# An attention and gated feed-forward block on one Trainium2 core: the second query block ends in half-width passes too, and the last one consists of them

## The chip, the cores and the metric

The kernel runs on one core of a Trainium2 chip. The metric is the device time of one execution in microseconds (us), as the median of several runs; lower is better. One execution was also taken by the hardware profiler, and its trace is what the text reads.

## The reference

One sequence of 2048 rows with 640 columns goes through a pre-normalized attention with 32 heads of 20 columns, and then through a gated feed-forward part with 1728 inner columns, all in bf16:

```python
qkv = (layernorm(x) @ wqkv)                      # 640 -> 3 x 640, 32 heads of 20
p = softmax(q @ k.T * 20 ** -0.5)                # per head, 2048 x 2048
h = x + (p @ v) @ wo
g, u = layernorm(h) @ w_gate, layernorm(h) @ w_up
h2 = h + (g * u) @ w_down
```

## The kernel before

**Attention.** The 32 heads are kept in 8 head groups (`NG`) of four, each head in a slot of 32 rows, so that four heads' score matmuls fill the 128 rows of TensorE. The 2048 queries are four blocks of 512 (`QB`), called 0 to 3. A *segment* is one head group's attention over all 16 key tiles for one *pass*, and a pass is a range of query columns: "0" to "3" are whole blocks, "C" and "D" are the two halves (256 columns, `HW`) of block 2, and "A" and "B" those of block 3. Blocks 0 and 1 are done in whole segments. Blocks 2 and 3 do their first two head groups (`SPLIT_G`) whole and the other six first for the left and then for the right half. Block 0's first four groups are done in four pieces of keys each, since the projections are still running then.

The segments' score columns are strung together and cut into *score tiles* of 1536 columns (three PSUM banks, `EW`); there are 683, the last one of 1024. The main loop runs over score tiles. For each, `emit_S` writes the score matmuls (L518), lets ScalarE take the Exp (L532) and may first let VectorE take the third bank with a polynomial of four instructions (`emit_x`, L562, L572, L573, L567), so that ScalarE's call is only 1024 columns wide. `x_takes` decides on that: the tile must lie in one segment and at least two tiles ahead of that segment's end, VectorE must not be behind by the planner's own clock, and in block 3 `room()` must find that the work still outstanding fits behind the remaining tiles. `emit_AV` (L716) multiplies the exponentials with the values some tiles later into one accumulator, which VectorE copies to `asb` (L728) when a segment ends.

**Normalizing.** A segment's sums of exponentials are inverted and spread over the rows of `asb` in one of two ways. `norm` goes by DRAM, with seven DMAs on SP's queue: `sums` (L616), `sums_all` (L617), and after a reciprocal on VectorE `scr` (L629) and four of `bc` (L632); POOL then multiplies (L638). `job_norm`, for the segments in `FAST`, goes by small matmuls on TensorE (L646, L662).

**The tail of a part.** When all head groups of a part (a whole block, or its left or right half) are normalized, `add_tail` queues its output projection (`job_out`: L953, with the sums for the second layer norm in `ln2_pieces`, then transposes into `ln2T`), the gated part (`job_glu`: `glu_sum` L1026 for 512 columns, `glu_pair` L1044 for 256 columns) and the down projection (`job_y`: L1090, four steps of 14 matmuls for two row tiles). Weights of the gated part come in seven slices of 256 columns; each is a pair of DMAs (`wu` and `wg`, L999, 320 KB each) into two buffers per name, called for one slice ahead of use. For block 3, slices 3 to 6 stay in the room that the queries leave free (`load_res`).

**Order.** All of this is put in order while the program is written. The planner keeps clocks of its own (`at`), and `run_job` fills the time that TensorE has left between two score tiles with steps of the queued jobs; `spare` does so with VectorE's steps (`aux`). `urgent` jobs go first. Where TensorE would be idle for long, `keep_warm` (L484) and `cool` (L514) write matmuls whose results nobody reads. Rows of `x` for a part are loaded early (`rows_early`) when the parts in `HELD_BY` have been stored. Each engine executes its own instructions in the order in which they were written, and so does SP with its DMAs.

**The end.** The tail of block 3's left half runs among the score tiles of its right half; what is left of it then is done in `last_tail`, which holds one of its four down projection steps back on purpose (`held`) and puts all leftovers (`fill()`) where TensorE waits for the last layer norm. Its order on TensorE is: output projection of the last two row tiles (`out_most`, L1188 and L1190) with the last normalization (L646, L662) in between, the leftovers (L1090), two transposes (L275), the gated part (L1026), and the down projection (L1090).

```python
    while i < n_tiles or av_q:
        ...
            rows_early(*due[0][2:])
        while due and normed(...):
            add_tail(*due.pop(0)[2:])
        if i < n_tiles:
            ran = run_job(max(at["exp"] - S_EXP - MARGIN, at["slot"][-2]))
```

Of the kernel before, what the change touches and what calls it, by code (L numbers as in the profile page):

```python
# [21 lines left out]
D = 640  # L22
H = 32
DH = 20
NT = S // P
# [4 lines left out]
NG = H // HPG  # L30
# [5 lines left out]
HW = QB // 2  # L36
# [3 lines left out]
FP = 7  # L40
FPW = 256
G1 = 4
SPLIT_G = 2
QA = 3 * QB
RES0 = 3
SM_SCALE = float(DH) ** -0.5
# [7 lines left out]
WAIT = "not yet"  # L54
# [27 lines left out]
def kernel(  # L82
# [17 lines left out]
    pool = lambda name, bufs=1, **kw: ctx.enter_context(tc.tile_pool(name=name, bufs=bufs, **kw))  # L100
# [44 lines left out]
    now = {"i": 0, "forced": False}  # L145
# [48 lines left out]
    def bn(mv, k, src, halves=None):  # L194
        st = small.tile([P, 2, 6], F32, name="st", bufs=4)
        for h in range(2):
            nc.vector.bn_stats(st[:, h, :], halves[h] if halves else src[:, h * HALF:(h + 1) * HALF])  # L197
        nc.vector.bn_aggr(mv[:, k, :], st[:])
# [39 lines left out]
    def ln_apply(dst, src, m32, r, k):  # L238
        nc.vector.tensor_scalar(dst, src, m32[:, k:k + 1], r[:, k:k + 1], ALU.subtract, ALU.mult)
# [17 lines left out]
    def evac(eng, dst, src):  # L257
        if eng == "act":
            nc.scalar.copy(dst, src)
        else:  # L260
            dve(690 if dst.dtype == BF16 and len(dst.shape) == 2 else 490)
            nc.vector.tensor_copy(dst, src)  # L262

    end = {"pool": None}

    def bank(dt=F32, w=BANK):
        if end["pool"] is None:
            return mip.tile([P, w], dt, name="mi", tag="mi")
        ps = end["pool"].tile([P, BANK], F32, name="f", tag="f")
        return ps if dt == F32 else ps[:].bitcast(dt)[:, 0:w]  # L270

    def job_T(ln, dst, eng="dve", ps=None, after=None):
        ps = bank(BF16, D) if ps is None else ps
        for c in range(KT):
            nc.tensor.transpose(ps[:, c * P:(c + 1) * P], ln[:, c * P:(c + 1) * P], ident[:])  # L275
        if after:
            after()
        evac(eng, dst, ps[:].rearrange("p (c k) -> p c k", k=P))
        yield 60 * KT
# [26 lines left out]
    def job_V(t, half):  # L306
        ps = bank()
        for c in range(KT):
# [8 lines left out]


    PASS = {"0": (0, 0, QB), "1": (1, 0, QB), "2": (2, 0, QB), "3": (3, 0, QB),
            "C": (2, 0, HW), "D": (2, HW, HW), "A": (3, 0, HW), "B": (3, HW, HW)}  # L320
    segs = []
    for ch in range(NB):
        for g in range(G1):
            kind = "copy" if ch == 0 else "last" if ch == NB - 1 else "add"
            segs.append(("0", g, ch * TPB, (ch + 1) * TPB, kind))
    segs += [("0", g, 0, NT, "only") for g in range(G1, NG)]
    segs += [("1", g, 0, NT, "only") for g in range(NG)]
    for full, halves in ("2", "CD"), ("3", "AB"):
        segs += [(full, g, 0, NT, "only") for g in range(SPLIT_G)]
        segs += [(p, g, 0, NT, "only") for p in halves for g in range(SPLIT_G, NG)]  # L330
    FINAL = len(segs) - 1
    TAILS = {0: [0], 1: [0], 2: [0, 2]}
    FAST = {("C", NG - 1), ("D", NG - 1), ("A", NG - 1), ("B", NG - 2)}

    tiles, cur_t, pos = [], [], 0
    for s, (p, g, lo, hi, _) in enumerate(segs):
# [23 lines left out]
    done = set()  # L360
# [4 lines left out]
    aux = deque()  # L365
# [72 lines left out]
    def step_aux():  # L438
        for gen in list(aux):
            try:  # L440
                c = next(gen)
                if c == WAIT:
                    continue
                at["dve"] += c or 200
                x_last[0] = None
                return True
            except StopIteration:
                aux.remove(gen)
        return False
# [11 lines left out]
    def ensure_aux(key):  # L461
        now["forced"] = True
        while key not in done:
            if not step_aux():
                raise RuntimeError(f"nothing makes {key}")
        now["forced"] = False
# [3 lines left out]
    full, partly = deque(), deque()  # L470
# [135 lines left out]
    def read_out(b):  # L606
        return all(("om", b, t) in done for t in TAILS[b])

# [74 lines left out]
    def emit_AV(upto):  # L683
# [40 lines left out]
        if acc["left"] == 0:  # L724
# [10 lines left out]
            if s == FINAL:  # L735
                final["asb"] = asb
            elif (p, g) in FAST:
                opens["nf", p, g] = at["dve"] + LAT
# [209 lines left out]
    def out_mm(on, st, t):  # L948
        for hf in range(2):
            ps = bank()  # L950
            cs = slice(hf * HALF, (hf + 1) * HALF)
            for g in range(NG):
                nc.tensor.matmul(ps[:, 0:HALF], lhsT=on[g][:, t * P:(t + 1) * P], rhs=wo[g][:, cs],  # L953
                                 start=(g == 0), stop=(g == NG - 1))
                if g == NG - 1:
                    dve(490)
                    nc.vector.tensor_tensor(st["h"][t][:, cs], ps[:, 0:HALF], st["xr"][t][:, cs], ALU.add)  # L957
                yield 136
            yield NEXT

    def ln2_pieces(st, ts, key):
        mv = small.tile([P, len(ts), 2], F32, name="mv")
        for k, t in enumerate(ts):
            bn(mv, k, st["h"][t][:])
            yield 1100
        made = []
        yield from rstd_steps(mv, len(ts), made, nc.gpsimd)
        for k, t in enumerate(ts):
            l_t = late["s"].tile([P, D], BF16, name="ln2")
            ln_apply(l_t[:], st["h"][t][:], *made[0], k)  # L970
            st["l", t] = l_t
            done.add(("l2", key, t))
            yield 440

    def job_out(on, st, ts, key):
        pairs = [ts[k:k + 2] for k in range(0, len(ts), 2)]

        def T_pair(pair):
            for t in pair:
                while ("l2", key, t) not in done and end["pool"] is None and key is not None:  # L980
                    yield WAIT
                ensure_aux(("l2", key, t))
                yield from job_T(st["l", t], st["ln2T"][:, :, t * P:(t + 1) * P])
                yield NEXT
        done.difference_update({("l2", key, t) for t in ts})
        for k, pair in enumerate(pairs):
            for t in pair:
                yield from out_mm(on, st, t)
            if key is not None and k == len(pairs) - 1:
                done.add(("om",) + key)  # L990
            if k:
                yield from T_pair(pairs[k - 1])
            aux.append(ln2_pieces(st, pair, key))
        yield from T_pair(pairs[-1])

    def w_tile(src, fp, wt):
# [111 lines left out]
    LAST_B, LAST_T = NB - 1, [2, 3]  # L1108

    rows_in = set()  # L1110
    HELD_BY = {(1, 0): [(0, 0)], (2, 0): [(0, 2)], (2, 2): [(1, 0)], (3, 0): [(1, 2)]}

    def rows(b, ts):
        if b not in tail_st:
            tail_st[b] = new_st(rows_of(b))
            tail_st[b]["res"] = late["res"]
        load_tail(tail_st[b], ts)
        rows_in.add((b, ts[0]))

    def rows_early(b, ts):  # L1120
        key = b, ts[0]
        if key in HELD_BY and key not in rows_in and all(("y",) + k in done for k in HELD_BY[key]):
            rows(b, ts)

    def add_tail(b, ts):
# [135 lines left out]
    def normed(p, gs):  # L1261
        return all(("n", p, g) in done for g in gs)

    n_tiles = len(tiles)
    first_last = next(k for k, (us, _) in enumerate(tiles) if PASS[segs[us[0][0]][0]][0] == LAST_B)
    due = [("0", range(NG), 0, [0, 1, 2, 3]), ("1", range(NG), 1, [0, 1, 2, 3]), ("C", range(SPLIT_G, NG), 2, [0, 1]),
           ("D", range(SPLIT_G, NG), 2, [2, 3]), ("A", range(SPLIT_G, NG), 3, [0, 1])]
    i = 0
    while i < n_tiles or av_q:
        now["i"] = i  # L1270
        if i < n_tiles:
            emit_S(i)
        else:
            while step_x():
                pass
        if i == first_last:
            for g in range(NG):
                ensure(("spill", g))
            load_res()
        if i == n_tiles:  # L1280
            root = small.tile([P, 1], BF16, name="root")
            nc.scalar.activation(root[:], ones[:], ACT.Sqrt)
        for _ in range(2):
            emit_AV(i if i >= n_tiles else i - 2 if i >= LAG else i - 3)
            if not av_q or min(u[0] for u in av_q) > i - E_BUFS + 1:
                break
        run_events(i)
        if due:
            rows_early(*due[0][2:])
        while due and normed(*due[0][0:2]) and (len(due[0][1]) == NG or normed(str(due[0][2]), range(SPLIT_G))):  # L1290
            add_tail(*due.pop(0)[2:])
        if i < n_tiles:
            ran = run_job(max(at["exp"] - S_EXP - MARGIN, at["slot"][-2]))
            idle = max(at["pe"], at["mi"]) + SWITCH + 2 * BANK * EXP_COL / 2
            if i > WARM and not ran and cur["fresh"] and idle < at["slot"][-2] + TOL:
                keep_warm()
                at["pe"] = idle
            spare(max(at["pe"], at["slot"][-2]))
        i += 1
# [103 lines left out]
```

## Time and profile before

| | |
|---|---|
| Median of 3 runs | 933.39 us (930.83 to 934.81) |
| The profiled execution | 932.5 us; its span, first to last instruction, 930.7 us |
| Mean granted TensorE clock | 0.997 |
| ScalarE busy | 875.8 us (94%), 719 instructions |
| TensorE busy | 823.8 us (89%); its weight loads 350.4 us |
| VectorE busy | 690.9 us (74%), 1289 instructions |
| POOL busy | 102.7 us (11%) |
| First Exp starts, last Exp ends | 15.5 us, 885.1 us |

The table is read against the span. An engine with a high share is not the limit at every moment: Exp runs from 15.5 to 885.1 us, and in the 45.6 us behind it ScalarE has little to do. TensorE's busy time counts the modelled ends of overlapping matmuls and keep-warm matmuls too.

### The profile page before, as it was taken

What the parts mean: (1) busy time and instruction counts of PE and PEld (TensorE: products, weight loads), DVE (VectorE), ACT (ScalarE), POOL (GpSimd) and SP (SyncE); (2) the same over time, 40 slices, a digit from 0 to 9 for tenths busy, and PEclk for the clock granted to TensorE, in tenths of its full rate; (3) what the DMA queues carried; (4) which work ended last, traced back from release to release, by engine and by line L of the source; (5) the groups of instructions that cost most, each with busy time, mean ns of one, the idle gap of its engine ahead of it and who ended that gap; (6) DMA issues with size and microseconds to landing.
All of it is one profiled execution on the core that took longest, in us unless ns stands there. A gap on an engine that the chain in (4) does not pass through costs nothing.

```text
span 930.7 us, 20159 instructions
## 1 busy us (share of the span) xinstructions
PE 823.8 (89%) x8046; PEld 350.4 (38%) x8115; DVE 690.9 (74%) x1289; ACT 875.8 (94%) x719; POOL 102.7 (11%) x293
## 2 busy tenths in 40 slices
PE   8788988889888898999898888999998999988897
PEld 5233332222223222233233333434434545435465
DVE  7674449898898888888898877887888886653242
ACT  6999999999999999999999999999999999999931
POOL 3310011000003200000013200020011000010000
PEclk9999999999999999999999999999999999999999
DMA  6000011011150032212400022112411221201210
GB/s 192 29 2 1 1 28 24 13 35 27 27 167 13 13 85 56 68 53 72 174 18 13 20 70 64 29 38 52 113 50 44 72 56 25 53 23 42 78 43 18
DMA packets 74204, 46.55 MB, mean 50 GB/s; under 512 B 20380, under 2 KB 70440, under 8 KB 74104
## 3 DMA queue, kind: packets, MB, share of 16 engines
q1 hardware_dynamic: 74104, 45.20, 17.8%
q8 instruction: 65, 1.06, 0.5%
q14 instruction: 35, 0.29, 0.1%
HBM read 37.88 MB, written 7.30 MB: 49 GB/s over the span
## 4 chain that ended last, share of the span: by engine, by line
ACT 43%; PE 30%; issue 15%; DVE 10%; POOL 1%; ACTq 0%; DVEq 0%
ACT E L532 43%; PE sc L518 7%; PE acc L716 4%; PE mi L1044 3%; PE mi L1090 3%; PE mi L1026 3%; PE mi L295 2%; PE f L1026 2%; PE f L1090 2%; PE mi L309 1%; DVE st L197 1%; DVE xt L572 1%; DVE hh L1051 1%; DVE u L1049 1%; DVE xt L573 1%
## 5 line engine op out<-in xcount | busy, mean ns | idle before, releaser
L532 ACT ACTIVATE E<-sc 128x1536 bf16<-128x1536 f32 (+1 forms) x683 | 858.2, 1383 | 11.9 <-PE sc L518 6.8
L518 PE MATMUL sc<-qa,kT 32*128 32x512 bf16 (+1 forms) x1920 | 202.1, 339 | 28.2 <-ACT E L532 18.7
L518 PEld LDWEIGHTS <-kT 32*128 32x128 bf16 x2816 | 83.3, 91 | 251.5 <-issue 214.7
L716 PE MATMUL acc<-E,vx 128*32 128x256 bf16 (+1 forms) x2598 | 169.5, 325 | 2.4 <-DVE asb L728 1.9
L562 DVE TENSOR_SCALAR xv<-sc 128x512 f32<-128x512 f32 x161 | 110.5, 688 | 39.1 <-PE sc L518 37.7
L572 DVE SCALAR_TENSOR_TENSOR xt<-xv 128x512 f32<-128x512 uint16 x161 | 112.6, 713 | 0.3
L573 DVE SCALAR_TENSOR_TENSOR xt<-xt,xv 128x512 f32<-128x512 f32 x161 | 112.0, 703 | 1.0
L567 DVE SCALAR_TENSOR_TENSOR xe<-xt,xv 128x512 int16<-128x512 f32 x161 | 111.0, 695 | 0.9
L638 POOL TENSOR_TENSOR on<-asb,bc 128x256 bf16<-128x256 f32 (+1 forms) x35 | 36.6, 1046 | 516.0 <-DMA bc<-scr 357.0
L295 PE MATMUL mi<-lnT,wp 128*128 128x512 bf16 x280 | 80.4, 381 | 12.1 <-DVE qa L302 3.4
L716 PEld LDWEIGHTS <-vx 128*32 128x32 bf16 x2816 | 57.4, 95 | 68.3 <-issue 67.7
L518 PE MATMUL sc<-qb,kT 32*128 32x256 bf16 (+1 forms) x896 | 68.6, 290 | 5.2 <-ACT E L532 4.1
L1090 PE MATMUL mi<-wd,hh 128*128 128x320 bf16 x350 | 62.0, 301 | 1.0 <-DVE xr L1094 0.9
L1090 PEld LDWEIGHTS <-hh 128*128 128x128 bf16 x448 | 38.4, 97 | 37.4 <-issue 25.5
L716 PE MATMUL acc<-xe,vx 128*32 128x256 bf16 (+1 forms) x218 | 48.2, 328 | 0.0
L1049 DVE CAST u<-mi 128x256 bf16<-128x256 f32 (+1 forms) x42 | 17.7, 422 | 38.0 <-PE mi L1044 37.6
L295 PEld LDWEIGHTS <-wp 128*128 128x128 bf16 x310 | 25.3, 97 | 54.7 <-issue 40.6
L514 PE MATMUL sc<-kT,ident 128*128 128x512 bf16 x74 | 28.4, 384 | 18.5 <-ACT E L532 17.7
L1026 PE MATMUL mi<-ln2T,wg 128*128 128x512 bf16 (+1 forms) x132 | 38.1, 382 | 4.3 <-DVE u L262 3.5
L953 PE MATMUL mi<-wo,on 128*128 128x320 bf16 x224 | 39.8, 301 | 2.1 <-DVE xr L957 1.8
L1026 PE MATMUL mi<-ln2T,wu 128*128 128x512 bf16 (+1 forms) x124 | 36.3, 382 | 4.7 <-DVE hh L1034 4.1
L1044 PE MATMUL mi<-ln2T,qa 128*128 128x256 bf16 (+1 forms) x240 | 33.5, 273 | 6.2 <-DVE hh L1051 5.4
(142 smaller groups left out, 667.6 us busy)
## 6 DMA issues: line engine op xcount, KB each, us to landing
wu<-in_B_w_up_dram SPq DMA_DIRECT2D x23, 320.0 KB
wg<-in_B_w_gate_dram SPq DMA_DIRECT2D x23, 320.0 KB
bc<-scr SPq DMA_DIRECT2D x80, 64.0 KB
qsp<-qa SPq DMA_DIRECT2D x8, 384.0 KB
xr<-in_A_x_dram SPq DMA_DIRECT2D x16, 160.0 KB
bc<-scr SPq DMA_DIRECT2D x76, 32.0 KB
out_dram<-xr SPq DMA_DIRECT2D x14, 160.0 KB
wd<-in_B_w_down_dram SPq DMA_DIRECT2D x13, 160.0 KB
```

The costliest lines, as they stand in the source:

```text
L295: nc.tensor.matmul(ps[:], lhsT=wslice(m, g, c), rhs=lnT[:, c, ch * QB:(ch + 1) * QB], start=(c == 0), stop=(c == KT - 1))
L518: nc.tensor.matmul(sc[:, o:o + w], lhsT=kT[g][SLOT * j:SLOT * (j + 1), kt * P:(kt + 1) * P], rhs=q_of(g, b, c0, w)[SLOT * j:SLOT * (j + 1) ...
L532: exps = nc.scalar.activation(e[:, 0:n_act], sc[:, 0:n_act], ACT.Exp, bias=EXP_BIAS, scale=SM_SCALE)
L562: took = nc.vector.tensor_scalar(v[:], ps, X_SCALE, X_BASE, ALU.mult, ALU.max)
L567: nc.vector.scalar_tensor_tensor(e[:], t[:], X_R, v[:], ALU.mult, ALU.add)
L572: lambda: nc.vector.scalar_tensor_tensor(t[:], u, X_P, u, ALU.add, ALU.mult),
L573: lambda: nc.vector.scalar_tensor_tensor(t[:], t[:], X_Q, u, ALU.add, ALU.mult),
L716: nc.tensor.matmul(acc["t"][SLOT * j:SLOT * (j + 1), 0:w], lhsT=vx[kt][:, VS * h:VS * h + SLOT], rhs=e, start=(acc["n"][j] == 0), stop=(ac ...
L953: nc.tensor.matmul(ps[:, 0:HALF], lhsT=on[g][:, t * P:(t + 1) * P], rhs=wo[g][:, cs], start=(g == 0), stop=(g == NG - 1))
L1026: nc.tensor.matmul(ps[0:M, 0:n], lhsT=st["w", fp][k][:, c, f2 * P:f2 * P + M], rhs=st["ln2T"][:, c, c0:c0 + n], start=(c == 0), stop=(c == ...
L1044: nc.tensor.matmul(ps[0:M, k * n:(k + 1) * n], lhsT=st["w", fp][k][:, c, f2 * P:f2 * P + M], rhs=st["ln2T"][:, c, c0:c0 + n], start=(c == ...
L1090: nc.tensor.matmul(ps[:, 0:HALF], lhsT=st["hh"][f][0:K, t * P:(t + 1) * P], rhs=late["Wd"][f][0:K, cs], start=(f == 0), stop=(f == 2 * FP ...
```

## The change

`SPLIT_G` becomes a number for each block: block 1 now does its first two head groups whole and the other six in halves, with the new passes "E" and "F"; block 2 stays as it was; block 3 has no whole segments, so all eight head groups are done for the left half and then for the right. Block 1's tail becomes two tails of two row tiles each. The last head groups of "E" and "F" are normalized by TensorE.

In `job_out`, the statistics of a pair of row tiles (`ln2_pieces`) are queued ahead of the transposes of the pair before it instead of behind them. `ln2_pieces` gets limits on how many pairs and normalized rows are open at once, and `T_pair` now also holds a part's transposes until the gated part that still reads the same columns of `ln2T` is written (`COLUMNS_OF`). `HELD_BY` changes with the new parts, and `rows_early` waits until the late pools are open.

```diff
--- before.py
+++ after.py
@@ -40,7 +40,7 @@
 FP = 7
 FPW = 256
 G1 = 4
-SPLIT_G = 2
+SPLIT_G = {"1": 2, "2": 2, "3": 0}
 QA = 3 * QB
 RES0 = 3
 SM_SCALE = float(DH) ** -0.5
@@ -317,20 +317,19 @@
 
 
     PASS = {"0": (0, 0, QB), "1": (1, 0, QB), "2": (2, 0, QB), "3": (3, 0, QB),
-            "C": (2, 0, HW), "D": (2, HW, HW), "A": (3, 0, HW), "B": (3, HW, HW)}
+            "E": (1, 0, HW), "F": (1, HW, HW), "C": (2, 0, HW), "D": (2, HW, HW), "A": (3, 0, HW), "B": (3, HW, HW)}
     segs = []
     for ch in range(NB):
         for g in range(G1):
             kind = "copy" if ch == 0 else "last" if ch == NB - 1 else "add"
             segs.append(("0", g, ch * TPB, (ch + 1) * TPB, kind))
     segs += [("0", g, 0, NT, "only") for g in range(G1, NG)]
-    segs += [("1", g, 0, NT, "only") for g in range(NG)]
-    for full, halves in ("2", "CD"), ("3", "AB"):
-        segs += [(full, g, 0, NT, "only") for g in range(SPLIT_G)]
-        segs += [(p, g, 0, NT, "only") for p in halves for g in range(SPLIT_G, NG)]
+    for full, halves in ("1", "EF"), ("2", "CD"), ("3", "AB"):
+        segs += [(full, g, 0, NT, "only") for g in range(SPLIT_G[full])]
+        segs += [(p, g, 0, NT, "only") for p in halves for g in range(SPLIT_G[full], NG)]
     FINAL = len(segs) - 1
-    TAILS = {0: [0], 1: [0], 2: [0, 2]}
-    FAST = {("C", NG - 1), ("D", NG - 1), ("A", NG - 1), ("B", NG - 2)}
+    TAILS = {0: [0], 1: [0, 2], 2: [0, 2]}
+    FAST = {("E", NG - 1), ("F", NG - 1), ("C", NG - 1), ("D", NG - 1), ("A", NG - 1), ("B", NG - 2)}
 
     tiles, cur_t, pos = [], [], 0
     for s, (p, g, lo, hi, _) in enumerate(segs):
@@ -958,7 +957,13 @@
                 yield 136
             yield NEXT
 
+    ln2 = {"open": 0, "rows": 0}
+    COLUMNS_OF = {(1, 0): (0, 0), (1, 2): (0, 0), (2, 0): (1, 0), (2, 2): (1, 2), (3, 0): (2, 0)}
+
     def ln2_pieces(st, ts, key):
+        while ln2["open"] >= 2 and not now["forced"]:
+            yield WAIT
+        ln2["open"] += 1
         mv = small.tile([P, len(ts), 2], F32, name="mv")
         for k, t in enumerate(ts):
             bn(mv, k, st["h"][t][:])
@@ -966,6 +971,10 @@
         made = []
         yield from rstd_steps(mv, len(ts), made, nc.gpsimd)
         for k, t in enumerate(ts):
+            while ln2["rows"] >= 2 and not now["forced"]:
+                yield WAIT
+            ln2["rows"] += 1
+            ln2["open"] -= k == len(ts) - 1
             l_t = late["s"].tile([P, D], BF16, name="ln2")
             ln_apply(l_t[:], st["h"][t][:], *made[0], k)
             st["l", t] = l_t
@@ -977,9 +986,11 @@
 
         def T_pair(pair):
             for t in pair:
-                while ("l2", key, t) not in done and end["pool"] is None and key is not None:
+                while end["pool"] is None and key is not None and (
+                        ("l2", key, t) not in done or key in COLUMNS_OF and ("glu",) + COLUMNS_OF[key] not in done):
                     yield WAIT
                 ensure_aux(("l2", key, t))
+                ln2["rows"] -= 1
                 yield from job_T(st["l", t], st["ln2T"][:, :, t * P:(t + 1) * P])
                 yield NEXT
         done.difference_update({("l2", key, t) for t in ts})
@@ -988,9 +999,9 @@
                 yield from out_mm(on, st, t)
             if key is not None and k == len(pairs) - 1:
                 done.add(("om",) + key)
+            aux.append(ln2_pieces(st, pair, key))
             if k:
                 yield from T_pair(pairs[k - 1])
-            aux.append(ln2_pieces(st, pair, key))
         yield from T_pair(pairs[-1])
 
     def w_tile(src, fp, wt):
@@ -1108,7 +1119,7 @@
     LAST_B, LAST_T = NB - 1, [2, 3]
 
     rows_in = set()
-    HELD_BY = {(1, 0): [(0, 0)], (2, 0): [(0, 2)], (2, 2): [(1, 0)], (3, 0): [(1, 2)]}
+    HELD_BY = {(1, 0): [], (1, 2): [(0, 0)], (2, 0): [(0, 2)], (2, 2): [(1, 0)], (3, 0): [(1, 2)]}
 
     def rows(b, ts):
         if b not in tail_st:
@@ -1119,7 +1130,7 @@
 
     def rows_early(b, ts):
         key = b, ts[0]
-        if key in HELD_BY and key not in rows_in and all(("y",) + k in done for k in HELD_BY[key]):
+        if key in HELD_BY and key not in rows_in and ("open",) in done and all(("y",) + k in done for k in HELD_BY[key]):
             rows(b, ts)
 
     def add_tail(b, ts):
@@ -1263,8 +1274,8 @@
 
     n_tiles = len(tiles)
     first_last = next(k for k, (us, _) in enumerate(tiles) if PASS[segs[us[0][0]][0]][0] == LAST_B)
-    due = [("0", range(NG), 0, [0, 1, 2, 3]), ("1", range(NG), 1, [0, 1, 2, 3]), ("C", range(SPLIT_G, NG), 2, [0, 1]),
-           ("D", range(SPLIT_G, NG), 2, [2, 3]), ("A", range(SPLIT_G, NG), 3, [0, 1])]
+    due = [("0", range(NG), 0, [0, 1, 2, 3]), ("E", range(SPLIT_G["1"], NG), 1, [0, 1]), ("F", range(SPLIT_G["1"], NG), 1, [2, 3]), ("C", range(SPLIT_G["2"], NG), 2, [0, 1]),
+           ("D", range(SPLIT_G["2"], NG), 2, [2, 3]), ("A", range(SPLIT_G["3"], NG), 3, [0, 1])]
     i = 0
     while i < n_tiles or av_q:
         now["i"] = i
@@ -1287,7 +1298,7 @@
         run_events(i)
         if due:
             rows_early(*due[0][2:])
-        while due and normed(*due[0][0:2]) and (len(due[0][1]) == NG or normed(str(due[0][2]), range(SPLIT_G))):
+        while due and normed(*due[0][0:2]) and (len(due[0][1]) == NG or normed(str(due[0][2]), range(SPLIT_G[str(due[0][2])]))):
             add_tail(*due.pop(0)[2:])
         if i < n_tiles:
             ran = run_job(max(at["exp"] - S_EXP - MARGIN, at["slot"][-2]))
```

## The prediction

> **What bounds the kernel now.** I read the page first, then the groups by form, the chain of waits, the timeline of the end, SP's own timeline and two tables of windows. In the costliest group of the page, ScalarE's Exp is busy for 858.2 of 930.7 us and idle for only 11.9 us in front of its 683 calls:
>
> ```profile
> L532 ACT ACTIVATE E<-sc 128x1536 bf16<-128x1536 f32 (+1 forms) x683 | 858.2, 1383 | 11.9 <-PE sc L518 6.8
> ```
>
> The groups by form split it (count, then busy us and mean ns, then idle time):
>
> ```profile
> L532 ACT ACTIVATE E<-sc 128x1536 bf16<-128x1536 f32 x521 | 722.5, 1483 | 10.1 <-PE sc L518 5.7 <-PE acc L716 2.3
> L532 ACT ACTIVATE E<-sc 128x1024 bf16<-128x1024 f32 x162 | 168.9, 1062 | 1.9 <-PE sc L518 1.1
> ```
>
> A 1024-wide call is one whose third bank VectorE took over (`x_takes`), except the last, which is a remainder. So time is worth something in two places: between 15.5 and 885.1 us, where only fewer Exp columns or fewer ScalarE waits count, and behind 885.1 us, where no Exp is left. There the chain of waits (start, us, what) is almost all TensorE:
>
> ```profile
> 885.51 1.30 PE mi L1090 x8
> 886.80 0.24 PE f L1188
> 887.04 0.95 PE f L1190 x7
> 887.99 0.34 PE f L646 x4
> ...
> 892.60 6.23 PE f L1090 x42
> 898.83 0.39 PE mi L275 x5
> ...
> 900.27 11.30 PE f L1026 x100
> ```
>
> The reader is to see that 8 + 42 matmuls of the down projection (L1090), left over from the last block's first part, stand on that path. The timeline shows what the 42 hide, the normalized rows of the last part:
>
> ```profile
> 894.73 1.12 DVE L1217 TENSOR_SCALAR ln<-f,m,rstd 128x320 bf16<-128x320 f32 x2
> 894.90 1.12 ACT L1218 ACTIVATE ln<-f,mr,rstd 128x320 bf16<-128x320 f32 x2 [0.48 <-DVE mr L1213]
> ```
>
> These are done at 896.02, and their transposes (L275) could start then, but start at 898.83.
>
> **Part 1, Exp.** The number of columns is fixed; what changes is VectorE's share. In the instruction order of the changed program the 1536-wide calls fall from 521 to 516, and the 1024-wide ones rise from 162 to 167. By query block the 1024-wide tiles go from 24, 54, 51, 33 to 24, 49, 49, 45: the half-width passes of block 1 lose some (a tile must lie in one head group and two tiles ahead of its end), and the last block gains 12, because less work is then outstanding in `room()`. 5 x (1483 - 1062) ns = -2.1 us, all on the path. VectorE pays 5 x (688 + 713 + 703 + 695) ns = 14.0 us, and some 8 us for narrower evacuations (PSUM copies: 8 of 684 ns become 16 of 420; GLU: 14 pairs of 688 + 687 become 28 of 422 + 424; small steps of the normalization). It is busy 690.9 us; the new x work lies mostly in the last block, where the windows 750 to 800 and 800 to 850 us have it busy for 32.5 and 28.5 of 50. Without that cover 22 us would be exposed; I take 0.
>
> **Part 2, the end.** In the changed order the 8 matmuls of L1090 ahead of the last output projection are gone, and 14 stand where 42 stood: the first part of the last block now comes after 8 half-width groups of that block instead of after 2 full and 6 half ones, so its down projection is finished but for the one half tile that is always held back. The last accumulator's copy ends at 886.02 and is needed only behind 1.19 us of L1188 and L1190, so the whole stretch moves by 1.30 us: the fill starts at 891.30 and takes 14/42 x 6.23 = 2.08 us, to 893.38. The normalized rows are now later than that: 896.02 - 1.30 = 894.72, with VectorE's at 894.55. Transposes at about 894.6 instead of 898.83: -4.2 us. Bounds: -1.3 if the normalization holds the transposes as late as its present slack allows, -5.5 (1.30 + 28/42 x 6.23) if nothing does; the rows above fix it near -4.2.
>
> **Part 3, TensorE.** 512 score matmuls of 512 columns become 1024 of 256. By the group rows 150.7/1152 = 131 ns against 2 x 51.4/768 = 134, so +1.5 us; AV 90 against 2 x 44.9, nothing; GLU 35.2/122 = 289 against 2 x 29.5/210 = 281, nothing. 42 fewer keep-warm matmuls (L484, L514) give room. All lies under 40.6 us in which TensorE waits for ScalarE (L518 22.9, L514 17.7): 0 on the path. POOL's multiplications go from 16 of 1.27 and 19 of 0.73 us to 8 and 33: nothing.
>
> **Part 4, SP's queue.** 64 more DMAs: six more normalizations by DRAM (7 each) and 22 more weight loads, because a GLU on half the columns reads the same weights. SP works in order (start, us):
>
> ```profile
> 843.41 0.50 SPq L616 DMA_DIRECT2D sums<-asb  x1
> 845.02 0.34 SPq L617 DMA_DIRECT2D sums_all<-sums  x1
> 845.46 0.40 SPq L999 DMA_DIRECT2D wu<-in_B_w_up_dram  x1
> 845.91 0.51 SPq L999 DMA_DIRECT2D wg<-in_B_w_gate_dram  x1
> 849.54 0.34 SPq L629 DMA_DIRECT2D scr<-ri  x1
> 851.37 1.72 SPq L632 DMA_DIRECT2D bc<-scr  x4
> ```
>
> A load behind a `sums` pair is issued 2.05 us after it; behind `scr` and four `bc` it would be 1.83 + 1.72 = 3.55 us. The windows (us, PE busy, clock, DMA share, GB/s) say when the pair of 845.46 has landed, at about 849.3, 3.9 us after issue:
>
> ```profile
> 848.40:849.40 1.00, 0.97 (x23) 1.00 0.77 200
> 849.40:850.40 1.00, 0.94 (x12) 1.00 0.01 0
> ```
>
> TensorE used it at 849.46 without a wait. In the changed order 16 such pairs are called for only 4 to 6 score tiles ahead of use, where before three were (6, 6 and 3). Four tiles of 1.33 us are 5.3 us; needed are 2.05 + 3.9 = 5.95 behind `sums`, 3.55 + 3.9 = 7.5 behind `bc`. So a pair waits for nothing (lower bound; a tile shortened by VectorE makes it worse, none makes it better) up to 2.2 us. A waiting LDWEIGHTS holds the score matmuls queued behind it, and ScalarE waits for those. I take two bad places of about 0.85 us, less some 0.3 us that TensorE is ahead (its waits for ScalarE are 22.9/62 = 0.37 us each): +1.1 us. The case of 849.46 is nearest, and it waited for nothing. The earlier statistics of block 0's second pair (`ln2_pieces` queued before the transposes) move VectorE and POOL work, with no change in count: 0. The extra waits in `T_pair` and the limits in `ln2_pieces` are decided while the program is written; they put no new semaphore wait on an engine beyond those of the order above.
>
> **Sum.** -2.1 - 4.2 + 1.1 = -5.2 us on a profiled execution of 932.5 (span 930.7 and 1.8 around it): 927.3. The median of the runs is 933.39, 0.9 above it: 928.2, -0.56%. 0.5% is 4.7 us, about the least that a measurement of this kernel can tell from no change.
>
> **Rival 1, slower: weight loads late behind SP's queue.** The mechanism of part 4 at each of the 16 pairs. At the bound of 2.2 us each it is 35 us on TensorE. It decides from 0.69 us per pair on ScalarE (5.2 + 4.7 + 1.1 = 11.0 us over 16): then 938 us. For it: 4 tiles are less than either sum. Against it: the buffers' last readers stand one to four tiles ahead of the call, and a pair with 3 tiles waited for nothing before. A milder form, 0.3 us per pair (4.8 instead of 1.1), leaves 931.9, no measurable change.
>
> **Rival 2, the clock.** TensorE's granted clock halves after a thin stretch, as these windows show:
>
> ```profile
> 672.50:675.90 3.40, 2.23 (x23) 1.00 1.16 297
> 675.90:679.30 3.40, 3.40 (x16) 0.50 0.38 104
> ```
>
> That cost ScalarE its longest wait (1.10 us). With the fill cut to a third, TensorE stands idle from 893.38 to 894.6 and again about 1.1 us between transposes and GLU, so 3.4 us at the end may be as thin; half a clock over the next 3.4 us of L1026 costs 1.7 us: 929.9. One more such stretch in the body, with 42 fewer keep-warm matmuls: 1.1 us more, 931.0. The Trainium skill (TensorE: Matmul & The Clock Gate, Why this matters for your kernels) speaks against shortening a fill: no idle gaps over about 3 us, or the clock falls to half. By that rule the gaps of 1.2 us would be harmless and the sum stays; the windows above, 66% busy and yet followed by half a clock, do not agree with it as a limit on idle time alone, so I keep this case.
>
> **Rival 3, nothing reaches the end.** If the 5 tiles only trade Exp for ScalarE waits (its 1024-wide calls are then followed by waits on the score slot), 2.1 us are lost and 930.3 remains.
>
> **Chances.** Forecast (-2.5 to -9) 0.60, of it 0.42 beyond -4.7; late weights, slower 0.13, mild 0.10; clock 0.10 (0.03 faster); rival 3 0.07. Faster 0.45, same 0.42, slower 0.13. The range: down to 924.5, if the four longest ScalarE waits of before (0.77, 0.77, 0.93, 1.10, together 3.6 us) do not come again; up to 937.0, late weights at 0.6 us per pair.
>
> **What would show it.** Exp 516 and 167 calls with the same means and idle time within 2 us of 11.9; in the chain L1090 x14 ahead of L275, no L1090 ahead of L1188, and from the last Exp's end to the span's end 41.4 instead of 45.6 us. Waits of L1044 on DMA of `wu` or `wg`, or on SP, of over 5 us would make the forecast wrong, and so would more than one half-clock stretch.

## The result and the profile after

| | before | changed |
|---|---|---|
| Median of 20 runs each | 933.20 us (930.01 to 935.89) | 936.52 us (934.03 to 941.64) |
| Ratio to before | | 1.0041, 95% interval 1.0026 to 1.0056 |
| Profiled execution, its span | 932.5, 930.7 us | 941.64, 939.8 us |
| First Exp starts, last Exp ends | 15.5, 885.1 us | 16.0, 896.4 us |
| From the last Exp's end to the span's end | 45.6 us | 43.4 us |

The change makes the kernel slower by 0.41%, where 0.56% faster was forecast. The changed kernel's profiled execution is the slowest of its 20 runs, so that its trace shows where time goes, while sizes are taken from the medians and ratios.

The changed line numbers are those of the new file: Exp is L531, scores L517, AV L715, the gated part of half a block L1055, the weight loads L1010. In the page of the profile Exp is about as busy as before (858.9 us against 858.2), and the idle time in front of it (the first number behind the second bar) has nearly doubled, from 11.9 us:

```profile
L531 ACT ACTIVATE E<-sc 128x1536 bf16<-128x1536 f32 (+1 forms) x683 | 858.9, 1375 | 22.2 <-PE sc L517 15.4
```

The groups by form show the forecast counts, 516 and 167, with means within 7 ns of the old ones:

```profile
L531 ACT ACTIVATE E<-sc 128x1536 bf16<-128x1536 f32 x516 | 715.7, 1478 | 14.9 <-PE sc L517 9.1 <-PE acc L715 3.5
L531 ACT ACTIVATE E<-sc 128x1024 bf16<-128x1024 f32 x167 | 172.8, 1055 | 7.3 <-PE sc L517 6.3
```

What is new among TensorE's waits (us in total, times, longest) is the weights; before had no such row:

```profile
PE mi L1055 <- DMA wu<-in_B_w_up_dram: 5.4, 4, 2.2
...
PE mi L1055 <- DMA wg<-in_B_w_gate_dram: 1.1, 3, 0.4
```

One of these waits, read on three views. SP's timeline: the load stands behind `scr` and four `bc`, and SP waits for `scr` to land before it may issue them (1.47 us from the start of `scr` to the first `bc`):

```profile
579.09 0.34 SPq L628 DMA_DIRECT2D scr<-ri  x1
580.56 1.73 SPq L631 DMA_DIRECT2D bc<-scr  x4
582.39 0.39 SPq L1010 DMA_DIRECT2D wu<-in_B_w_up_dram  x1
582.88 0.47 SPq L1010 DMA_DIRECT2D wg<-in_B_w_gate_dram  x1
```

TensorE's timeline: the up weights of the slice are used as soon as they are there, 3.3 us after their issue, and the score matmuls are behind them:

```profile
585.71 0.72 PE L1055 MATMUL mi<-ln2T,wu 128*128 128x256 bf16 x5 [1.12 <-DMA wu<-in_B_w_up_dram]
586.78 0.40 PE L1055 MATMUL mi<-ln2T,wg 128*128 128x256 bf16 x1 [0.35 <-DMA wg<-in_B_w_gate_dram]
587.11 0.62 PE L517 MATMUL sc<-qa,kT 32*128 32x256 bf16 x6
```

The table of windows (us, TensorE busy, clock, DMA share, GB/s) shows what follows: the stretch with the wait is thin, and half a clock comes behind it. The last two lines show the same at the end of the kernel:

```profile
582.30:585.70 3.40, 2.08 (x40) 1.00 0.68 191
585.70:589.10 3.40, 3.04 (x22) 0.63 0.28 54
589.10:592.50 3.40, 3.40 (x34) 0.50 0.60 172
...
904.00:907.40 3.40, 1.61 (x15) 1.00 0.07 24
907.40:910.80 3.40, 3.40 (x17) 0.51 0.82 217
```

At the end 14 leftover matmuls of the down projection stand where 42 stood, as TensorE's timeline shows:

```profile
902.46 2.17 PE L1101 MATMUL f<-wd,hh 128*128 128x320 bf16 x14
```

The chain of waits now runs through VectorE's normalized rows, as forecast, and the gated part takes 12.97 us there instead of 11.30, for the half clock:

```profile
904.83 1.05 DVE ln L1228 x2
905.88 0.05 issue
905.92 0.34 PE mi L275 x3
...
907.33 12.97 PE f L1037 x100
```

### The profile page after: what moved, and what is told of

Read it like the earlier page. It is cut to its first block, busy times and chain, and to the rows that moved or that the text cites. A ratio compares the mean times of both kernels' runs of the same rounds, so it can differ in the third digit from the quotient of the medians.

```text
span 939.8 us, 22688 instructions
## 1 busy us (share of the span) xinstructions
PE 837.4 (89%) x9253; PEld 381.8 (41%) x9253; DVE 710.9 (76%) x1359; ACT 876.4 (93%) x719; POOL 100.9 (11%) x299
## 4 chain that ended last, share of the span: by engine, by line
ACT 41%; PE 32%; issue 13%; DVE 11%; DMA 2%; SPq 0%; ACTq 0%; DVEq 0%
ACT E L531 40%; PE sc L517 7%; PE acc L715 6%; PE mi L1055 5%; PE mi L1101 4%; PE mi L1037 2%; PE f L1037 2%; PE mi L295 2%; DMA wg<-in_B_w_gate_dram 1%; DVE u L1060 1%; DVE hh L1062 1%; PE mi L483 1%; DVE xt L572 1%; PE mi L309 1%; DVE xt L571 1%
## 5 line engine op out<-in xcount | busy, mean ns | idle before, releaser
L531 ACT ACTIVATE E<-sc 128x1536 bf16<-128x1536 f32 (+1 forms) x683 | 858.9, 1375 | 22.2 <-PE sc L517 15.4
L517 PE MATMUL sc<-qa,kT 32*128 32x256 bf16 (+1 forms) x2304 | 204.5, 311 | 22.6 <-ACT E L531 15.8
L517 PEld LDWEIGHTS <-kT 32*128 32x128 bf16 x3328 | 85.3, 92 | 231.9 <-issue 193.5
L715 PE MATMUL acc<-E,vx 128*32 128x256 bf16 (+1 forms) x3047 | 171.0, 303 | 2.6 <-DVE asb L727 2.1
L566 DVE SCALAR_TENSOR_TENSOR xe<-xt,xv 128x512 int16<-128x512 f32 x166 | 117.0, 709 | 0.9
L715 PEld LDWEIGHTS <-vx 128*32 128x32 bf16 x3328 | 74.3, 96 | 70.2 <-issue 68.9
L517 PE MATMUL sc<-qb,kT 32*128 32x256 bf16 x1024 | 68.9, 274 | 3.0 <-ACT E L531 2.2
L1101 PE MATMUL mi<-wd,hh 128*128 128x320 bf16 x378 | 68.5, 302 | 1.5 <-DVE xr L1105 1.5
L1055 PE MATMUL mi<-ln2T,wu 128*128 128x256 bf16 (+1 forms) x270 | 40.2, 278 | 15.5 <-DVE hh L1062 8.6
L1060 DVE CAST u<-mi 128x256 bf16<-128x256 f32 x70 | 29.4, 420 | 32.5 <-PE mi L1055 31.5
L715 PE MATMUL acc<-xe,vx 128*32 128x256 bf16 (+1 forms) x281 | 51.9, 295 | 0.0
L1055 PE MATMUL mi<-ln2T,wg 128*128 128x256 bf16 (+1 forms) x270 | 46.9, 281 | 1.1 <-DMA wg<-in_B_w_gate_dram 1.1
L302 DVE TENSOR_SCALAR kT<-mi,one_row 128x512 bf16<-128x512 f32 x30 | 22.3, 744 | 20.5 <-PE mi L295 20.3
L1055 PEld LDWEIGHTS <-wu 128*128 128x128 bf16 (+1 forms) x270 | 24.7, 99 | 30.1 <-issue 20.4
```

What stands on the lines that cost most here:

```text
L517: nc.tensor.matmul(sc[:, o:o + w], lhsT=kT[g][SLOT * j:SLOT * (j + 1), kt * P:(kt + 1) * P], rhs=q_of(g, b, c0, w)[SLOT * j:SLOT * (j + 1) ...
L531: exps = nc.scalar.activation(e[:, 0:n_act], sc[:, 0:n_act], ACT.Exp, bias=EXP_BIAS, scale=SM_SCALE)
L566: nc.vector.scalar_tensor_tensor(e[:], t[:], X_R, v[:], ALU.mult, ALU.add)
L715: nc.tensor.matmul(acc["t"][SLOT * j:SLOT * (j + 1), 0:w], lhsT=vx[kt][:, VS * h:VS * h + SLOT], rhs=e, start=(acc["n"][j] == 0), stop=(ac ...
L1055: nc.tensor.matmul(ps[0:M, k * n:(k + 1) * n], lhsT=st["w", fp][k][:, c, f2 * P:f2 * P + M], rhs=st["ln2T"][:, c, c0:c0 + n], start=(c == ...
L1060: nc.vector.tensor_copy(u[0:M, 0:n], ps[0:M, 0:n])
```

## The experiments

Theory A is that waits for weight loads cost what the forecast left out, mostly because the loads stand behind the normalization's DMAs in SP's queue. Rivals: the clock falls because 42 keep-warm matmuls are gone (B), or half-width matmuls cost more than their rows say (C). Ratios are to the kernel before, run on the same chip; each interval is 95%.

**No loads (e1).** All instructions on TensorE, ScalarE and VectorE stand as in the changed kernel; pairs of loads are left out, so part of the gated result uses other weights. The profile has 19 pairs into the `wu` and `wg` buffers instead of 36, so 17 pairs are gone; the expectation below counts 22.

```diff
+                if ("w", nx) not in st and nx > 1 and n <= HW and end["pool"] is None:
+                    st["w", nx] = st["w", 1]
                 if ("w", nx) not in st:
                     load_w(nx, st)
```

> The changed kernel, with the half-width gated parts using weight slice 1 for slices 2 to 6 as well, so that 22 pairs of weight loads are left out (that part of the result is computed with other weights). TensorE, ScalarE and VectorE get the same instructions in the same order. Theory A (waits of TensorE for weight loads, and the half clock that follows such a wait, cost what the forecast left out): no wait of L1055 on a DMA, at most two half-clock stretches, Exp's excess back near that of before, 926 to 929 us, ratio to before about 0.995. Theory B (the clock falls because 42 keep-warm matmuls are gone, loads or not): several half-clock stretches stay, 934 to 938 us. Theory C (half-width scores and values cost more than their group rows say): no half-clock stretches, yet 934 us or more.

Measured: 929.96 us, 0.9956 (0.9939 to 0.9973), no wait on a weight DMA. The idle time in front of Exp, by form:

```profile
L531 ACT ACTIVATE E<-sc 128x1536 bf16<-128x1536 f32 x516 | 715.8, 1482 | 12.2 <-PE sc L517 6.8 <-PE acc L715 3.4
L531 ACT ACTIVATE E<-sc 128x1024 bf16<-128x1024 f32 x167 | 173.2, 1058 | 2.5 <-PE sc L517 1.4
```

That is 14.7 us against 22.2. So the loads cost 1.0041 - 0.9956 = 0.85%, 7.9 us (by the two intervals, some 2 us more or less). B and C would have kept the time at 934 or more. The clock isn't lower without the keep-warm matmuls either: nine of e1's 12 runs have a mean clock of 0.996 or more, of the kernel before on the same chip 11 of 35.

**A third buffer for the up weights (e2).** The loads stay; `wu` is called two slices ahead (for room, `u` has one buffer and `st` three).

```diff
+            for nx in order[k + 2:k + 3]:
+                if ("w", nx) not in st and ("u", nx) not in st and ...:
+                    load_u(nx, st)          # name="wu", bufs=3
```

> The changed kernel with three buffers instead of two for the up weights, called two slices ahead; the gate weights stay at one slice ahead. Same order on TensorE, ScalarE and VectorE. Theory A: waits on wu go from 5.4 us to 0, those on wg stay under 2 us because a single load lands sooner, 928 to 931 us, ratio about 0.997. Theories B and C: 935 to 938 us, ratio about 1.004.

Measured: 930.51 us, 0.9965 (0.9947 to 0.9983); 1.8 us of waits on weights are left in the profile, 1.4 of them on `wg`. All loads are still made, here and in e3, so it isn't their traffic that costs the time.

**SP's queue relieved (e3).** No buffer more, no call sooner; only the DMAs that make SP wait are issued later.

```diff
-        nc.sync.dma_start(r16, sums[:]...)
+        later(2, lambda: nc.sync.dma_start(r16, sums[:]...))
...
-            bc = nrm.tile(...); four dma_start(bc[...], scr[...])
+            def spread():
+                bc = at_bc["t"] = nrm.tile(...); four dma_start(bc[...], scr[...])
+            later(2, spread)
```

> The changed kernel with SP's queue relieved: sums_all is issued two score tiles after sums, and the four bc two tiles after scr, so that SP doesn't stand waiting for them while a weight load is behind them. Loads are called where they were. Theory A with SP's queue as the delay: a load is issued 1.6 us sooner behind sums and 1.5 to 3.5 us sooner behind scr, waits of L1055 on DMA fall from 6.5 us to under 2, 929 to 932 us, ratio about 0.998. Theory A with the short lead alone as the delay: no change, 936 us. Theories B and C: no change, 936 us.

Measured: 929.04 us, 0.9951 (0.9934 to 0.9968), no wait on a weight DMA in the profile. SP's timeline at the place shown above has the load behind `scr` alone, 2.86 us sooner:

```profile
579.08 0.34 SPq L628 DMA_DIRECT2D scr<-ri  x1
579.53 0.37 SPq L1014 DMA_DIRECT2D wu<-in_B_w_up_dram  x1
580.00 0.48 SPq L1014 DMA_DIRECT2D wg<-in_B_w_gate_dram  x1
580.57 1.86 SPq L634 DMA_DIRECT2D bc<-scr  x4
```

So with SP's queue relieved the short lead is enough, and with a longer lead (e2) the queue does no harm: it is the two together that made the loads late.

**Keep-warm matmuls at the end (e4).** Six matmuls of 512 columns behind `fill()`.

```diff
         fill()
+        warm_ps = bank()
+        for _ in range(6):
+            nc.tensor.matmul(warm_ps[:], lhsT=ident[:], rhs=kT[0][:, 0:BANK], start=True, stop=True)
```

> The changed kernel with six keep-warm matmuls of 512 columns behind the leftover down projection at the end, where TensorE otherwise stands until the last layer norm is done. They take about 1.3 us of a gap of 2.5 us. If the half clock at 907.4 us comes from that gap, it doesn't come here, and the stretch from the last Exp's end to the span's end falls from 43.4 to 41.7 us in runs that had it; the median falls by 0.5 to 1.7 us, to 935 us, ratio about 1.003. If it has another cause, no change, 936.5 us.

Measured: 935.58 us, 1.0026 (1.0005 to 1.0047). In its profile the stretch behind the last Exp takes 41.3 us and has no half clock. The ratio lies 0.15% under the changed kernel's, but the intervals overlap: not told apart. The runs of e1 to e3 that were profiled had no half clock there either (41.3 to 41.8 us), so the gap doesn't always bring it.

**Block 1's halves alone (e5), block 3's halves alone (e6).**

```diff
-SPLIT_G = {"1": 2, "2": 2, "3": 0}
+SPLIT_G = {"1": 2, "2": 2, "3": 2}     # e5
+SPLIT_G = {"1": 8, "2": 2, "3": 0}     # e6, with TAILS, HELD_BY, COLUMNS_OF and due for block 1 as one part
```

> The changed kernel with block 3 split as before (2 whole head groups), so that block 1's halves are the only new ones. 163 Exp calls are 1024 wide (before 162, changed 167), and 8 and 42 leftover matmuls of the down projection stand in the tail as before: the two gains of the forecast are gone, the 13 tight pairs of weight loads in block 1's and 2's gated parts are there. Theory A: waits of L1055 on DMA of 3 to 5 us in the profile, 938 to 941 us, ratio 1.006 to 1.009, slower than the whole change. If the waits came with block 3's halves instead: 933 us.

Measured: 937.72 us, 1.0045 (1.0031 to 1.0060), 2.8 us of waits on weights in the profile; time, ratio and waits are all a little under the ranges expected, and the ratio isn't told apart from that of the whole change.

> The changed kernel with block 1 whole as before, so that block 3's halves are the only new ones. 160 Exp calls are 1024 wide, 42 leftover matmuls stand in the tail, only four pairs of weight loads are tight. Theory A: hardly a wait on weights, and no gain either, because the work that was to be done sooner is still behind block 2: 933 to 935 us, ratio about 1.001. If block 3's halves carry the gain by themselves: 928 us.

Measured: 933.53 us, 0.9996 (0.9976 to 1.0016), 1.0 us of waits. Its profile has 160 calls of 1024 columns and 42 leftover matmuls, as expected; only the 8 ahead of the last output projection are gone, and the stretch behind the last Exp takes 44.2 us. So the 12 tiles that VectorE takes more of, and the shorter leftover, need block 1 and block 3 together; of the gain at the end 1.4 us come with block 3 alone. Of the cost, block 1 alone brings 0.45%, 4.2 us, and block 3 alone none that shows. The rest of the 7.9 us comes only with both, and why isn't shown.

**All three remedies (e7).** e2, e3 and e4 in one kernel.

> The changed kernel with the third buffer for the up weights, SP's queue relieved and six keep-warm matmuls at the end, together. Theory A: no wait of L1055 on DMA, 41.3 us from the last Exp's end to the span's end, 927 to 929 us, ratio 0.994, the best so far; the half clock near 386 us, in the thin stretch behind pass E's last segment, is not touched and stays in part of the runs.

Measured: 928.83 us, 0.9950 (0.9931 to 0.9969). Nothing that shows is gained over e3; 1.2 us of small waits on `wu` are back in its profile. Both e3 and e7 are faster than the kernel before and than the changed one.

**The relief in the kernel before (e8).** The edit of e3 on the old kernel.

> The kernel before with SP's queue relieved in the same way. Theory A: nothing waits for a weight load there, so no change, 933 us, ratio 0.999 to 1.001. If the relief helps by something else than weights (normalization sooner): as much as in the changed kernel, 929 us.

Measured: 932.80 us, 0.9990 (0.9974 to 1.0006). The relief is worth nothing that shows where no load is tight.

**The order of the statistics alone (e9).** `SPLIT_G` = {"1": 8, "2": 2, "3": 2}, with the entries of e6 for block 1.

> The changed kernel with blocks 1 and 3 split as before, so that only the order of the statistics, the holds in T_pair and ln2_pieces and the new condition of rows_early are left of the change. The counts of Exp calls, leftovers, keep-warm matmuls and DMAs are those of before. Theory A: no change, 933 us, ratio 0.999 to 1.001. If the statistics' new place costs VectorE or POOL time where block 0's second pair waits: up to 935 us.

Measured: 934.37 us, 1.0005 (0.9987 to 1.0022). What the change does beside the splits of blocks 1 and 3 makes no difference that shows.

**The same wait put into the kernel before (e10).** The next slice is called half a slice later.

```diff
-            for nx in order[k:k + 2]:
-                if ("w", nx) not in st:
-                    load_w(nx, st)
+            if ("w", fp) not in st:
+                load_w(fp, st)
             for f2 in range(2):
+                if f2:
+                    for nx in order[k + 1:k + 2]:
+                        if ("w", nx) not in st:
+                            load_w(nx, st)
```

> The kernel before with each weight pair called half a slice later, so that 13 pairs are called 2 to 6 score tiles ahead of use instead of 3; nothing else is changed on TensorE, ScalarE or VectorE. Theory A: waits on DMA of wu appear in L1026 and L1044, 3 to 8 us in the profile, 937 to 941 us, ratio 1.004 to 1.009, like the changed kernel. If the changed kernel lost its time by something that only comes with its half-width passes: 933 us, no waits.

Measured: 938.29 us, 1.0048 (1.0029 to 1.0067), with waits where there were none, at 573.7 and 707.1 us:

```profile
PE mi L1044 <- DMA wu<-in_B_w_up_dram: 1.7, 1, 1.7
...
PE mi L1026 <- DMA wu<-in_B_w_up_dram: 1.1, 1, 1.1
```

The old kernel becomes as slow as the changed one by the late calls alone, without any new half-width pass. The profile, of the fastest of its seven runs, has 14.5 us of idle time in front of Exp instead of 12.0; where the rest of the 4.5 us lies isn't shown.

## Why the prediction was wrong

**Part 1 held in its count, but the time didn't come.** 516 and 167 calls of the old means make the -2.1 us, yet the row of both forms together has Exp busy for 858.0 us in e1 against 858.2 before. That fits calls that overlap when they follow each other without a wait (12 of them, of 1483 ns on average, take 16.00 us in the timeline before, from 869.05 on) and don't behind one. In e1 the idle time also grew by 2.7 us over the 12.0 of before: half a clock for 6.8 us from 385.6 us on, behind a thin stretch after pass E's last segment, and 3.4 instead of 2.3 us of waits for the accumulator's matmuls. How much of that is in every run isn't settled. By its ratio e1 gained 4.1 us where parts 1 and 2 had 6.3, so 2.2 us are missing, the size of rival 3; that the waits are those that rival 3 named isn't shown.

**Part 2 held.** 45.6 us became 41.3 to 41.8 in e1 to e4 and e7, where 41.4 was forecast; in the changed kernel's own profile it is 43.4, by the 1.7 us of rival 2.

**Part 3 and the statistics.** e9 shows no cost of the statistics. e1 leaves part 3 at most the 2.2 us that are missing, and no run takes those apart.

**Part 4 is the term that was mis-sized.** It named the mechanism, took "two bad places of about 0.85 us, less some 0.3 us", +1.1 us, and the term measured 7.9 us by e1. The 6.8 us between the two and the 2.2 us missing from part 1 make up the 9.0 us (0.97%) between forecast and result. Three steps of the term failed. First the places: the profile has five, at 519, 586, 676, 709 and 848 us, and in four of them TensorE waits 0.9 to 2.2 us for `wu` (at 676 only for `wg`, 0.35 us); the row taken as nearest, a pair with 3 tiles that waited for nothing, had 4.0 us between issue and use, while the one at 585.71 had 2.2 us until TensorE stood ready. What counts is the time from the issue on, so the lead less the time for which SP holds the load back. At the longest wait, 2.21 us at 709.47, SP held it back for longer than the 3.55 us of the prediction: 5.32 us from `scr` to `wu`, since the first `bc` came only 3.5 us behind `scr`:

```profile
700.84 0.34 SPq L628 DMA_DIRECT2D scr<-ri  x1
704.34 1.72 SPq L631 DMA_DIRECT2D bc<-scr  x4
706.16 0.39 SPq L1010 DMA_DIRECT2D wu<-in_B_w_up_dram  x1
```

Then the 0.3 us: ScalarE lost the whole wait, 1.67 us at 521.2 for TensorE's 1.14 + 0.38. Last the clock: rival 1 and rival 2 were priced apart, but a wait can make the thin stretch behind which the clock is halved, so that around 586 us TensorE's 1.47 us of waiting, 1.51 us to ScalarE, were followed by 0.49 and 1.34 us more of ScalarE waits.

Both signs of a wrong forecast came: 6.5 us of waits on weights, and more than one half-clock stretch (from about 153, 587, 710 and 907 us on). The clock is not the main part, though. Among the changed kernel's 20 runs, the seven with a mean clock of 0.996 or more took 934.0 to 935.5 us, the eight with 0.992 or less 936.6 to 941.6; e1's nine runs of 0.996 or more lie between 927.5 and 931.4. The means of these seven and nine are 934.7 and 929.4, so about 5.3 of the 7.9 us are there at the same clock. And the clock falls without late loads too: e3's profile, of its slowest run and with no wait on weights, has half a clock from about 32, 387 and 789 us on. The rule of the Trainium skill that rival 2 cites (TensorE: Matmul & The Clock Gate, Why this matters for your kernels) names idle gaps of over about 3 us between bursts of matmuls as what to avoid. This case's trace has half a clock without such a gap: the longest single waits ahead of it were 1.12 us at 585.71 and 0.78 us, twice, around the last transposes.

**Chances.** The median came out 0.41% slower, inside what the text called no change, to which it gave 0.42, though the interval lies clear of 1, and it is above the likeliest value by 8.3 us and close to the end of the range. Most of it was rival 1 between its milder form and the one that decides (0.3 and 0.69 us per pair were priced; 7.9 us over 16 pairs are 0.49).

## What to carry to other kernels

When a part is cut in halves, its weights are read twice in the same time, so each load has about half the time, while it takes as long as before: price the lead in us against the whole way of the load, and that begins with what its issuing queue waits for ahead of it. A DMA that waits for another DMA belongs into an in-order queue only when its wait is over; moving two kinds of such issues two tiles later was worth as much as leaving 17 pairs of loads out. And a wait that leaves a thin stretch on TensorE is to be priced together with the half clock that can follow it.

## What was not expected of the hardware

Half a clock followed stretches of 3.4 us in which TensorE was busy for 2.29 us (e1, 382.20 to 385.60), 2.08 us (582.30 to 585.70) and 1.61 us (904.00 to 907.40), with no single wait longer than 1.12 us in them. The busy time alone doesn't decide: in the changed kernel's profile the stretch from 382.20 to 385.60 has the same 2.29 us, and the clock behind it stays at 1.00. What else decides isn't shown.

A load of 320 KB of up weights was usable 3.3 us after its issue in three places (issued at 582.39, 706.16 and 844.53, used at 585.71, 709.47 and 847.83), and the gate load behind the first of them 3.9 us after its own issue (582.88 to 586.78).
